# Attention and a gated feed-forward on one core: w_in without its scaling copy, the first job's probabilities kept in float32, four blocks of x turned by TensorE, and a new order

## The chip, the core and the metric

The kernel runs on one core of a Trainium2 chip. A core has five engines that run side by side: TensorE (PE in the profile, with its weight loads as PEld), VectorE (DVE), ScalarE (ACT), GpSimd (POOL) and SyncE (SP), which here issues nearly all the transfers. The metric is device time in microseconds (us), lower is better.

## What is computed

The reference takes q, k and v of four batches, eight heads, 1152 rows and 64 columns, and two matrices of a feed-forward network.

```python
q_pool = q.reshape(B, H, S // 2, 2, D).mean(axis=3)
scores = (1 / sqrt(D)) * q_pool @ k.T            # 576 x 1152 a head
attn = softmax(scores)
x = concat_heads(attn @ v)                       # 2304 x 512
h = x @ w_in                                     # 512 -> 2048
out = (h * sigmoid(h)) @ w_out                   # 2048 -> 512
```

Inputs and output are float32. Most products are made in float16, with each operand split into a high part and a rest ("hi" and "lo"), so that three float16 products stand for one of nearly float32 precision.

## The kernel before

**Jobs.** Attention goes by pairs of heads (16 pairs, four a batch). A job is one pair and one chunk of 128 pooled query rows: its two sides are the two heads. A batch has four whole chunks for each pair, and a job of the 64 rows left over for every two pairs: 72 jobs, numbered from 0 here. For each side, TensorE makes the scores into a PSUM tile S (L723), VectorE takes the row maximum (L784, tile nm), and ScalarE the exponential with the row's sum (L800, tile p32, "p" in the profile). There is one S buffer for each side, so that a job's scores can only begin when the exponentials of the job before are done. The first four pairs, which are those of jobs 0 to 17, have their scores made in float32.

**Turning p.** The product with v needs p turned. As a rule p is split into hi (a cast on ACT at L408 or on DVE at L412) and lo (a subtraction at L432 on POOL or DVE), tile phl, and the two halves go through DMA transposes that SP issues (L827), into pt. For side 1 of jobs 0 to 3 TensorE turns p itself: nine float32 transposes into PSUM tiles pp (L841), from which ACT copies hi (L687) and DVE subtracts lo (L432, pt<-pp). Either way 27 float16 products per side follow (L935, tile po). `whole`, which turns a side and keeps it in float32, is in the kernel before but not used.

**Weights.** w_in and w_out come in 32 pieces of 128x512 (16 each), as 64-bit words; ACT and DVE rebuild the float32 value in place (tiles wide and raw): the low word (L613 on ACT or L619 on DVE), a scaled copy into a PSUM tile mm (L606), and the joining of the two on DVE (L634). For w_in a scaling copy in place follows (the `more` step), and for both the hi part (a cast to the weight tile w, by ACT, DVE or POOL) and the lo part (a subtraction at L432 on POOL or DVE).

**Blocks.** When the jobs of a chunk are done, its 128 rows of x are a block. For the first two blocks TensorE turns x (L1064, tile px), and ACT or DVE takes hi (L690 for DVE) and DVE lo (L1085) from PSUM. For the others x is split into xs (ACT or DVE, then POOL or DVE) and turned by a DMA transpose (L1044). A block has 192 products with w_in (L1130), the gate on ACT and DVE (tiles t and g), and 48 with w_out (L1225). 18 blocks in all.

**What sets the order.** All steps are entered in a plan (`Plan.add`) with a cost, a priority, and the tiles that they hold; `Plan.order` then lists them once, at build time, as if each engine took the ready step of least priority number, with a rule for which engine takes a step that several may do. The list is the program: on the chip every engine works through its own instructions in that order, and so does the SP queue. The priorities and the rules' weights are the tables PRI, PRE, W, EV and the constants above them. Steps that use the SBUF ports that DVE and POOL share are entered with port=True.

## Time and profile before

| what | value |
|---|---|
| median of 3 runs | 714.14 us (712.02 to 714.36) |
| the profiled execution | 714.45 us, its span 712.5 us |
| TensorE busy | 653.3 us, 92% of the span |
| ScalarE, VectorE, GpSimd busy | 480.4, 471.9 and 463.9 us, 66 to 67% |
| mean granted clock of TensorE | 0.976 |

The span runs from the first instruction to the last; the execution's own time is 1.95 us longer. All terms below are worked out against the profiled execution, which is 0.31 us above the median. A share of busy time over the whole span mixes stretches that have different limits, so the profile has to be read in stretches: the first 130 us, where TensorE is often idle, and the rest, where it hardly is.

### The profile page before, as it was taken

How to read it: one execution, taken by the hardware profiler on the slowest of the kernel's cores; microseconds unless marked ns; L12 is line 12 of the kernel's file. 1: busy time of each engine (PE TensorE's matmuls, PEld its weight loads, DVE VectorE, ACT ScalarE, POOL GpSimd, SP SyncE). 2: the span in 40 equal slices, each digit the busy share in tenths (PEclk: the TensorE clock that was granted, in tenths of full speed). 3: DMA queues.
4: the chain of work that ended last, by engine and by line, in shares of the span. 5: the costliest groups of instructions: out<-in, count | busy, mean ns of one | idle time of the engine just before them, and what ended most of it. 6: DMA issues, size and time to landing. Idle time of an engine off the chain costs nothing. (4 is left out here: it accounts for less than half of the span.)

```text
span 712.5 us, 23295 instructions
## 1 busy us (share of the span) xinstructions
PE 653.3 (92%) x10052; PEld 470.7 (66%) x10052; DVE 471.9 (66%) x839; ACT 480.4 (67%) x707; POOL 463.9 (65%) x260
## 2 busy tenths in 40 slices
PE   4656877999899999999899999998999999999997
PEld 2333655676767686767486868585868686858767
DVE  5878885689678575776678756586777565754111
ACT  4978977997577665777655766695777675865221
POOL 1657985897437776778635867887579776666111
PEclk8788999999999999999999999999999999999999
DMA  8999899999999999999999999999999999999000
GB/s 347 358 283 246 159 205 225 238 195 212 200 303 177 163 182 168 161 247 194 207 255 172 180 181 166 167 252 176 280 218 172 184 173 157 159 175 158 24 16 16
DMA packets 362886, 138.10 MB, mean 194 GB/s; under 512 B 350112, under 2 KB 350368, under 8 KB 362784
## 3 DMA queue, kind: packets, MB, share of 16 engines
q1 hardware_dynamic: 362624, 136.49, 99.6%
q8 instruction: 78, 1.28, 0.7%
q14 instruction: 24, 0.20, 0.1%
q10 hardware_dynamic: 160, 0.13, 0.1%
HBM read 45.09 MB, written 4.72 MB: 70 GB/s over the span
## 5 line engine op out<-in xcount | busy, mean ns | idle before, releaser
L432 POOL TENSOR_TENSOR phl<-p,phl 128x1152 f16<-128x1152 f32 x119 | 291.6, 2457 | 100.6 <-DVE phl L412 58.6
L800 ACT ACTIVATE p<-S,nm 128x1152 f32<-128x1152 f32 x144 | 174.8, 1215 | 99.1 <-DVE nm L791 46.5
L784 DVE TENSOR_REDUCE nm<-S 128x1 f32<-128x1152 f32 x144 | 194.5, 1351 | 53.2 <-PE S L723 52.9
L1130 PE MATMUL mm<-xt,w 128*128 128x128 f16 x3456 | 203.6, 220 | 4.8 <-DVE raw L634 2.1
L1130 PEld LDWEIGHTS <-w 128*128 128x128 f16 x3456 | 195.5, 98 | 11.1 <-DMA xt<-xs 2.5
L1225 PE MATMUL mm<-w,g 128*128 128x512 f16 x816 | 186.5, 380 | 2.1 <-DVE nm L791 1.9
L432 POOL TENSOR_TENSOR g<-t,g 128x512 f16<-128x512 f32 x72 | 98.4, 1368 | 80.4 <-ACT g L408 79.6
L723 PE MATMUL S<-K,Q 64*128 64x512 f16 (+7 forms) x1320 | 138.2, 373 | 13.4 <-ACT p L800 6.7
L935 PE MATMUL po<-V,pt 128*128 128x64 f16 (+1 forms) x4320 | 130.8, 195 | 20.0 <-DMA pt<-phl 9.8
L935 PEld LDWEIGHTS <-pt 128*128 128x128 f16 (+1 forms) x4320 | 122.3, 102 | 32.4 <-issue 12.7
L1225 PEld LDWEIGHTS <-g 128*128 128x128 f16 x816 | 75.9, 98 | 85.7 <-issue 2.5
L408 ACT ACTIVATE phl<-p 128x1152 f16<-128x1152 f32 x99 | 114.4, 1160 | 8.2 <-DMA pt<-phl 5.8
L1151 DVE SCALAR_TENSOR_TENSOR t<-t,mm 128x512 f32<-128x512 f32 x72 | 49.3, 684 | 59.8 <-ACT t L1144 57.6
L723 PEld LDWEIGHTS <-Q 64*128 64x128 f16 (+1 forms) x1080 | 42.2, 97 | 51.3 <-issue 11.1
L1144 ACT ACTIVATE t<-mm 128x512 f32<-128x512 f32 x72 | 42.5, 591 | 23.0 <-PE mm L1130 22.7
L408 ACT ACTIVATE g<-t 128x512 f16<-128x512 f32 x72 | 45.1, 627 | 18.0 <-DVE t L1151 17.9
L761 DVE TENSOR_SCALAR r<-sum 128x1 f32<-128x1 f32 (+1 forms) x152 | 17.1, 147 | 50.5 <-ACT p L800 50.1
L723 PEld LDWEIGHTS S<-K,Q 64*128 64x128 f32 (+1 forms) x240 | 23.2, 211 | 39.4 <-issue 24.2
L412 DVE CAST phl<-p 128x1152 f16<-128x1152 f32 x41 | 33.7, 822 | 9.9 <-DMA pt<-phl 7.1
L432 POOL TENSOR_TENSOR xs<-x,xs 128x512 f16<-128x512 f32 (+1 forms) x16 | 19.8, 1238 | 24.3 <-ACT xs L408 24.1
L432 DVE TENSOR_TENSOR phl<-p,phl 128x1152 f16<-128x1152 f32 x21 | 32.1, 1533 | 4.4 <-ACT phl L408 4.2
L535 DVE SCALAR_TENSOR_TENSOR V<-ld,V 128x1152 f16<-128x1152 f32 x16 | 27.6, 1729 | 6.6 <-ACT V L408 6.6
(59 smaller groups left out, 390.7 us busy)
## 6 DMA issues: line engine op xcount, KB each, us to landing
ld<-q SPq DMA_DIRECT2D x16, 576.0 KB, 5.7
ld<-v SPq DMA_DIRECT2D x16, 576.0 KB, 6.1
ld<-k SPq DMA_DIRECT2D x12, 576.0 KB, 6.4
pt<-phl SPq DMA_TRANSPOSE x280, 4.3
wide<-w_in SPq DMA_DIRECT2D x8, 512.0 KB, 8.8
wide<-w_out SPq DMA_DIRECT2D x8, 512.0 KB, 7.9
raw<-w_in SPq DMA_DIRECT2D x8, 512.0 KB, 4.9
raw<-w_out SPq DMA_DIRECT2D x8, 512.0 KB, 5.4
```

The source lines that it names most:

```text
L408: nc.scalar.activation(out=out(), in_=src(), func=AF.Copy, scale=scale or 1.0)
L412: nc.vector.tensor_copy(out=out(), in_=src())
L432: return lambda: getattr(engine, op)(out=out(), in0=a(), in1=b())
L535: lambda: nc.vector.scalar_tensor_tensor(out=values(1), in0=v3(), scalar=V_SCALE, in1=values(0)[:, :, :D], op0=ALU.mult, op1=ALU.subtract,),
L723: nc.tensor.matmul(o[to, c], lhsT=a[rows, s], rhs=x[rows, c], start=n == 0, stop=n == len(terms) - 1,)
L784: lambda: nc.vector.tensor_reduce(out=nm(), in_=ps()[:, :S], op=ALU.max, axis=AX.X),
L800: lambda: nc.scalar.activation(out=p32(), in_=ps()[:, :S], func=AF.Exp, scale=0.0625, bias=nm(), **({} if SUM_BY_PE else dict(accum_out=sm ...
L935: nc.tensor.matmul(o[to, keep : keep + n], lhsT=pt[:, hl * NK + c, cols], rhs=vv[:, at : at + n], start=c == 0 and hl + vl == 0, stop=c == ...
L1130: nc.tensor.matmul(o, lhsT=w[:, f // 2 % 4, wl, cols], rhs=moving(xl, kk), start=kk == 0 and wl + xl == 0, stop=kk == 3 and wl == 1,)
L1144: lambda: nc.scalar.activation(out=t(), in_=h(), func=AF.Tanh, scale=1.0 / G_SCALE),
L1151: lambda: nc.vector.scalar_tensor_tensor(out=t(), in0=t(), scalar=1.0, in1=h(), op0=ALU.add, op1=ALU.mult,),
L1225: nc.tensor.matmul(o(), lhsT=g[ff // 4]()[:, gl, ff % 4], rhs=w[:, u % 4, wl, e * DM : e * DM + DM], start=ff == ffs[0] and gl + wl == 0, ...
```

## The change

Three edits go with a new set of the planner's tables, and thus with another order of everything.

1. `MORE = False`: the scaling copy of the 16 w_in pieces is left out. The cast to hi takes the scale along, and lo, which was a subtraction on POOL or DVE, is now scalar times value minus hi, one instruction on DVE alone (`LO_BY`).
2. `SIDES32 = 2`: both sides of job 0 go through `whole`. TensorE turns p in float32, ACT or DVE copies it once, and nine float32 products with v as it was loaded take the place of the 27 float16 ones. Side 0 had gone by hi, lo and two DMA transposes; side 1 by nine transposes, hi and lo.
3. `X_BY_PE = 4`: blocks 2 and 3 of x are turned by TensorE, too.

The planner has a new constant `LATE`, which lets it count on the result of a DMA transpose later, and new costs for a few steps. `T_IN_PSUM` is set so that the step at L606 stays as it was.

```diff
-WAIT = 0.189
-AHEAD, SWITCH, STEAL = 1.286, 21.317, 1.144
+WAIT = 0.183
+LATE = 0.781
+AHEAD, SWITCH, STEAL = 3.441, 215.979, 1.229
...
-MORE = True
+LO_BY = ("dve",)
+MORE = False
...
-X_BY_PE = 2
-SIDES32 = 0
+X_BY_PE = 4
+SIDES32 = 2
+T_IN_PSUM = True
...
-            at = max(at, b.end + (0.0 if same else LATENCY[b.engine]))
+            at = max(at, b.end + (0.0 if same else LATENCY[b.engine]) + (LATE if b.moves == "turn" else 0.0))
...
             if more != 1.0:
-                add(
-                    "dve", slow,
-                    lambda: nc.vector.scalar_tensor_tensor(
+                def lo_on(engine):
+                    return lambda: engine.scalar_tensor_tensor(
                         out=w()[:, u % 4, 1, c], in0=value(), scalar=more, in1=hi(),
                         op0=ALU.mult, op1=ALU.subtract,
-                    ),
+                    )
+
+                either(
+                    [x for x in (("dve", slow, lo_on(nc.vector)), ("pool", pool_cost(512), lo_on(nc.gpsimd))) if x[0] in LO_BY],
                     pr + W["lo"], [("raw", *tok), ("whi", *tok)], [("wlo", *tok)], [raw, w],
                 )
...
                 if by_32(j, i):
                     add(
-                        "pe", 9 * 4 * pe_cost(64) + 0.1,
+                        "pe", 2.02,
```

Three places of the new order matter below. In the names, the numbers tell buffers apart.

On the SP queue, after the loads of the first three pairs; before:

```order
L595 DMA wide_129<-w_in 128x1024 x2
L595 DMA wide_129<-w_out 128x1024
L827 DMA_TRANSPOSE pt_175<-phl_161 128x9x128 x2
L474 DMA ld_201<-q 128x1152
L474 DMA K_204<-k 128x1152
L474 DMA ld_215<-v 128x1152
L595 DMA wide_129<-w_out 128x1024
```

and after, at the same place:

```order
L599 DMA wide_129<-w_in 128x1024 x2
L599 DMA wide_129<-w_out 128x1024 x2
L477 DMA ld_175<-q 128x1152
L477 DMA K_181<-k 128x1152
L477 DMA ld_191<-v 128x1152
L599 DMA raw_208<-w_in 128x1024
```

The two transposes of job 0's side 0 are gone, and the loads of the fourth pair (q, k, v) follow the weights directly.

On TensorE, from the last transpose of job 0's side 1 (p_21) on; before, with the scores of job 2 in S_52 and S_53:

```order
L841 MATMUL pp_189<-one_84,p_21_134 128x128
L841 MATMUL pp_220<-one_84,p_43_212 128x128 x4
L841 MATMUL pp_230<-one_84,p_43_212 128x128 x4
L723 MATMUL S_52_242<-K_101,Q_137 128x512
L723 MATMUL S_53_243<-K_101,Q_137 128x512
```

and after, with the scores of job 2 in S_56 and S_57:

```order
L884 MATMUL pp_189<-one_84,p_21_134 128x128
L884 MATMUL pp_195<-one_84,p_25_146 128x128 x4
L884 MATMUL pp_203<-one_84,p_25_146 128x128 x4
L884 MATMUL pp_216<-one_84,p_25_146 128x128
L930 MATMUL po_224<-ld_91,pt_210 128x64 x9
L930 MATMUL po_224<-ld_91,pt_155 128x64 x9
L730 MATMUL S_56_264<-K_101,Q_137 128x512
```

The nine transposes of side 0 (p_25) and the 18 float32 products of job 0 now stand ahead of job 2's scores; the transposes of job 1's side 1 (p_43 before) have moved behind them.

On VectorE, from the reciprocal of job 0's sums to the row maxima of job 1; before:

```order
L773 RECIPROCAL r_157<-r_157 128x2
L412 CAST phl_161<-p_25_146 128x1152
L432 TENSOR_TENSOR pt_155<-pp_141,pt_155 128x512
L432 TENSOR_TENSOR pt_155<-pp_150,pt_155 128x512
L634 SCALAR_TENSOR_TENSOR wide_107<-mm_180,wide_107 128x512
L535 SCALAR_TENSOR_TENSOR V_163<-ld_105,V_163 128x1152
L634 SCALAR_TENSOR_TENSOR wide_107<-mm_184,wide_107 128x512
L432 TENSOR_TENSOR pt_155<-pp_189,pt_155 128x128
L784 TENSOR_REDUCE nm_198<-S_32_166 128x1
```

and after:

```order
L780 RECIPROCAL r_157<-r_157 128x2
L538 SCALAR_TENSOR_TENSOR V_161<-ld_105,V_161 128x1152
L639 SCALAR_TENSOR_TENSOR wide_107<-mm_177,wide_107 128x512
L639 SCALAR_TENSOR_TENSOR wide_107<-mm_183,wide_107 128x512
L791 TENSOR_REDUCE nm_193<-S_31_164 128x1
L798 TENSOR_SCALAR nm_193<-nm_193 128x1
L791 TENSOR_REDUCE nm_214<-S_30_163 128x1
L798 TENSOR_SCALAR nm_214<-nm_214 128x1
L661 SCALAR_TENSOR_TENSOR w_0_36_185<-wide_107,w_0_36_185 128x512 x2
```

Job 0's cast and its three lo subtractions are gone, and the new lo instructions of w_in (L661) have come in behind the row maxima of job 1.

## Rows read from the trace of the kernel before

**Rows 1.** The page: busy time of TensorE, and its busy tenths in 40 slices.

```profile
PE 653.3 (92%) x10052; PEld 470.7 (66%) x10052; DVE 471.9 (66%) x839; ACT 480.4 (67%) x707; POOL 463.9 (65%) x260
...
PE   4656877999899999999899999998999999999997
```

**Rows 2.** Busy time by stretch: us, the engines, then clock, DMA share, GB/s.

```profile
10.00:60.00 50.00, 29.11 (x264) 18.73 (x260) 42.59 (x79) 42.00 (x70) 27.64 (x19) 0.80 1.07 333
60.00:100.00 40.00, 30.89 (x446) 21.67 (x444) 33.72 (x60) 36.29 (x57) 36.10 (x22) 0.91 0.95 181
100.00:130.00 30.00, 23.33 (x348) 17.29 (x347) 19.35 (x37) 22.17 (x35) 21.13 (x13) 0.94 1.13 222
130.00:200.00 70.00, 66.71 (x1036) 46.84 (x1033) 52.29 (x89) 53.19 (x81) 50.07 (x30) 0.98 1.15 216
200.00:650.00 450.00, 440.65 (x7180) 318.30 (x7179) 313.20 (x562) 309.32 (x440) 312.47 (x160) 1.00 1.09 194
```

**Rows 3.** What TensorE waited for in the first 150 us: us, times, longest.

```profile
PE pp L841 <- ACT p L800: 12.6, 4, 4.5
```

**Rows 4.** Groups of instructions, first 150 us: count, busy us, mean ns, idle before.

```profile
L432 POOL TENSOR_TENSOR phl<-p,phl 128x1152 f16<-128x1152 f32 x23 | 56.3, 2456 | 24.7 <-DVE phl L412 14.9 <-ACT phl L408 9.7
...
L408 ACT ACTIVATE phl<-p 128x1152 f16<-128x1152 f32 x16 | 18.4, 1158 | 1.3 <-DMA pt<-phl 1.2
...
L432 POOL TENSOR_TENSOR w<-wide,w 128x512 f16<-128x512 f32 x14 | 16.3, 1177 | 4.8 <-ACT w L408 4.7
...
L606 ACT ACTIVATE mm<-wide 128x512 f32<-128x512 f32 x16 | 9.8, 631 | 0.0
...
L412 DVE CAST phl<-p 128x1152 f16<-128x1152 f32 x9 | 7.5, 837 | 3.9 <-DMA pt<-phl 3.9
...
L408 ACT ACTIVATE wide<-wide 128x512 f32<-128x512 f32 x7 | 4.7, 677 | 1.2 <-DVE wide L634 1.2
...
L417 POOL TENSOR_SCALAR wide<-wide 128x512 f32<-128x512 f32 x1 | 0.6, 641 | 0.1
```

**Rows 5.** DVE instructions by line: count, min/median/max ns (three answers).

```profile
L535 DVE SCALAR_TENSOR_TENSOR V<-ld,V x4: 1348/1377/2308, 8.8 to 35.8; 128x1152 f16<-128x1152 f32 x4
...
L432 DVE TENSOR_TENSOR Q<-ld x2: 750/754/757, 4.8 to 10.1; 128x576 f32<-128x576 f32 x2
L432 DVE TENSOR_TENSOR w<-wide,w x2: 1544/1614/1683, 81.9 to 84.5; 128x512 f16<-128x512 f32 x2
L432 DVE TENSOR_TENSOR w<-raw,w x1: 686/686/686, 91.5 to 91.5; 128x512 f16<-128x512 f32 x1
L432 DVE TENSOR_TENSOR phl<-p,phl x1: 1352/1352/1352, 124.2 to 124.2; 128x1152 f16<-128x1152 f32 x1
...
L619 DVE TENSOR_SCALAR raw<-raw x2: 428/1510/2592, 38.8 to 39.2; 128x512 uint32<-128x512 uint32 x2
```

**Rows 6.** TensorE in order of time: start, us, what [idle before].

```profile
25.33 1.97 PE L841 MATMUL pp<-one,p 128*128 128x128 f32 x8 [4.54 <-ACT p L800]
27.23 3.98 PE L723 MATMUL S<-K,Q 64*128 64x512 f32 x12
...
98.73 0.60 PE L1064 MATMUL px<-one,x 128*128 128x128 f32 x4
...
115.82 2.84 PE L1130 MATMUL mm<-xt,w 128*128 128x128 f16 x48 [0.42 <-DVE x L1007]
...
130.38 2.75 PE L1225 MATMUL mm<-w,g 128*128 128x512 f16 x12 [0.28 <-DVE t L1151]
133.06 2.21 PE L723 MATMUL S<-K,Q 64*128 64x512 f32 x12
```

**Rows 7.** TensorE's weight loads for the float32 transposes, first 60 us, ns.

```profile
L841 PEld LDWEIGHTS pp<-one,p x36: 139/225/231, 14.3 to 52.8; 128*128 128x128 f32 x36
```

**Rows 8.** The SP queue in order of time.

```profile
16.97 8.61 SPq L827 DMA_TRANSPOSE pt<-phl  x2
```

**Rows 9.** ACT's wait on a weight load, 10 to 100 us.

```profile
ACT wide L613 <- DMA wide<-w_in: 1.4, 1, 1.4
```

More of the change, by code (lines that the diff above doesn't have):

```diff
@@ L150, in add @@
         tiles = [x for t in tiles for x in (t, t.share) if x is not None]
-        op = Op(options, priority, tiles, port, moves, matmuls, mode, spare)
+        op = Op(options, round(priority, 4), tiles, port, moves, matmuls, mode, spare)
         before = []
@@ L581, in halves, with carried @@
                 return bits().bitcast(F16).rearrange("p (a b) -> p a b", b=4)[:, :, j]
-            def tu():
-                return t().bitcast(U32)
             def value():
                 return words(1)
+            def carried():
+                return t() if T_IN_PSUM else words(1)
             def hi():
@@ L625, in weights @@
                 "act": ("act", act_cost(512) + 0.02, low_act),
[L626 removed]
+                "dve": ("dve", dve_cost(512, True) + 0.08, low_on(nc.vector)),
             }
@@ L629, in weights @@
                 [ways[x] for x in LOW_BY],
-                pr + W["low"], writes=[("low", *tok)], reads=[("raw", *tok)], tiles=[raw],
+                pr + W["low"], writes=[("low", *tok)], reads=[("raw", *tok) if T_IN_PSUM else ("came", *tok)], tiles=[raw],
             )
@@ L634, in weights @@
                 lambda: nc.vector.scalar_tensor_tensor(
-                    out=words(1).bitcast(U32), in0=tu(), scalar=3, in1=words(0).bitcast(U32),
+                    out=words(1).bitcast(U32), in0=carried().bitcast(U32), scalar=3, in1=words(0).bitcast(U32),
                     op0=ALU.logical_shift_left, op1=ALU.bitwise_or,
                 ),
-                pr + W["put"], [("low", *tok), ("t", *tok)], [("raw", *tok)], [t, raw], port=False,
+                pr + W["put"], [("low", *tok), ("t", *tok)], [("raw", *tok)], [*scratch, raw], port=not T_IN_PSUM,
             )
```

33 lines of the change are left out of this document (17 added, 16 removed).

## The prediction

> **What bounds the kernel now.** I read the page's busy row and its slices first, then the busy time by stretch, then TensorE's waits, and last the groups of instructions. The busy row alone would say that TensorE sets the time at 92%, but the slices show where the missing 8% lie: they are low up to about the seventh and near nine tenths from there to the end [rows 1]. By stretch, TensorE is idle for 20.9 of the 50 us from 10 to 60, for 9.1 of the 40 up to 100, for 6.7 of the 30 up to 130, then for 3.3 of 70 and 9.4 of 450 [rows 2]. From 130 us on it is thus the bound, and whatever it has not done by then is added at the end. Ahead of that it waits, most of all for the exponentials that its float32 transposes need, 12.6 us in four waits [rows 3]. No single engine holds it there: from 10 to 60 VectorE and ScalarE are busy for 85 and 84% and GpSimd for 55%; from 60 to 100 they are at 84, 91 and 90% [rows 2]. The start-up is work of three engines that pass pieces to each other, and GpSimd becomes a bound in its second part.
>
> The mark that I use is the start of job 13's scores, at 133.06 us [rows 6]: ahead of it TensorE is idle often, behind it hardly. The end moves by two things: by how much earlier this mark is reached, and by how much more of TensorE's own work is done when it is.
>
> **What the new order has done by the mark.** Counted in the two orders, TensorE has 48 more products with w_in (288 for 240) and 12 more with w_out (48 for 36) ahead of job 13's scores, and as many jobs' products with v. 48 of the first took 2.84 us and 12 of the second 2.75 [rows 6], together 5.6 us that no longer have to be done behind the mark.
>
> The other engines' work up to the row maximum, the exponential and the split of job 13, as counts by durations:
>
> ScalarE: 9 copies in place fewer, at 0.68 us, -6.1 [rows 4] (all 13 scaling copies that it had go, but more of the low words now stand ahead of the mark); 5 casts to hi fewer, at the same 0.68, -3.4; 4 scaled copies into PSUM more, at 0.63, +2.5; 3 casts of p more, at 1.16, +3.5 [rows 4]; three copies of turned p, x and pieces of the gate more, seven in all at about 0.6 each (the 0.63 of its PSUM copies is the nearest row), +4.0. Sum +0.5.
>
> VectorE: the 16 new lo instructions. Its free subtraction of this size took 0.69 [rows 5], so +11.0; 4 joinings and gates more of that size, +2.8; 4 casts of p fewer, at 0.84, -3.4 [rows 4]; job 0's three lo subtractions, one of w and one copy of x fewer, some 3.1. Sum +7.3.
>
> GpSimd: 12 subtractions of w fewer, at 1.18, -14.1; 3 scaling copies fewer and 9 casts to hi more, at 0.64, +3.8; one subtraction of p fewer, at 2.46, -2.5 [rows 4]; one of the gate more and one of x fewer, 0. Sum -12.8.
>
> Together -5.0 us of work. From 10 to 130 us the three engines did 95.7, 100.5 and 84.9 us of it, 281 in 120 [rows 2], or 2.34 us for each us of time. If they go on at that rate the mark comes 2.1 us earlier. The bounds: if VectorE alone set the pace (it was busy for 80% of the 120 us), its 7.3 us cost 9.2; if GpSimd alone did (71%), its 12.8 give back 18. I take the mean rate, since no engine was the bound throughout.
>
> **What else is added.** The new lo instructions read two operands from SBUF, as the lo step of v does, and that one took 2.31 us for 1.35 where GpSimd was at work beside it [rows 5]. Of the ten two-operand SBUF instructions that VectorE ran in the first 150 us (four on v, three on w, two on q, one on p), three were so held up, v once by 0.96 and w twice, to 1.54 and 1.68 for 0.69 [rows 5]; that is 2.8 us over ten, 0.28 each. For sixteen this is 4.5 us of VectorE, and at 2.34 a us of time 1.9. The longest hold that the trace shows is 2.16 (2.59 for 0.43, a low word) [rows 5], so the range for all sixteen runs from nothing to 34.6 us of VectorE.
>
> The Trainium skill, SBUF — State Buffer, Who interferes with whom, says that a VectorE instruction with two SBUF inputs and a GpSimd one that reads SBUF exclude each other for the whole of the one that came first. The trace agrees, by the 2.31 us above. Taken as chance meetings with a GpSimd that is busy 71% of the time from 10 to 100 us and in the middle of a 2.46 us subtraction, the rule would give an estimate of 0.87 us a hold and a time of 712.2 instead of the forecast below; I hold to the measured 0.28, because it is of this kind of order.
>
> Job 0. Side 0 loses its cast, its subtraction and two DMA transposes. SP stood at those from 16.97 to 25.58, and the fourth pair's loads only went out behind them [rows 8]; now they follow the weights. What this gives back is bounded by nothing below (no engine is shown to wait for the q or k of that pair) and by the waits on loads: ScalarE's 1.4 us for a piece of w_in [rows 9]. I take the 1.4, since a queue without the two transposes lets those pieces go out earlier, too. TensorE gets nine transposes (eight took 1.97 at the low clock [rows 6]) and 18 float32 products for 54 float16 ones. The trace has no such product; its float32 weight loads took 139 to 231 ns, median 225 [rows 7], so by those 18 cost 2.5 to 4.2 us, and twice as much, 8.4, if the load is not what counts and the clock is low (scores took 3.98 at 27 us and 2.21 at 133 [rows 6]). They stand ahead of job 2's scores, which wait behind them, and so do the row maxima of job 2. I cost them at nothing: TensorE sat idle for 4.54 us just there, from 20.8 to 25.3, until job 1's exponentials [rows 6], and had no other work. If that cover is gone or the clock is low, they delay the start-up by up to 4 us. Below nothing they can't go: what they spare the other engines is counted above.
>
> Blocks 2 and 3 of x: eight transposes, which come behind the mark, where TensorE is the bound. Four took 0.60 in the midst of other work [rows 6]: +1.2. The split and the two DMA transposes that go lie beside TensorE's work, where the other engines are busy for 70 to 75% [rows 2], and count for nothing.
>
> Behind 200 us the counts of each engine barely change, TensorE was idle for 9.4 of 450 us [rows 2], and the new order may make that a few us more or less: 0, with 3 either way.
>
> **The sum.** -5.6 (work done earlier) -2.1 (three engines) +1.9 (holds) -1.4 (transfers) +1.2 (x) = -6.0. From 714.45 that is 708.45; the median of the runs stood 0.31 lower, so 708.1.
>
> **Rivals.**
>
> VectorE becomes the bound (slower). It is the one engine that gets work, 7.3 us and the holds, up to the mark. Against it: it was idle for a fifth of the time there, and the row maxima depend on TensorE and ScalarE. For it: 84 to 85% up to 100 us [rows 2]. Then 7.3 and 4.5 us come at 80% busy: 14.8 us later, less 5.6 and 1.4 and with 1.2: 723.1. In holds alone: each us of mean hold costs 16 / 2.34 = 6.8 us, the sum without holds is 706.5 for the profiled execution, and so this alone makes it slower by over 0.3% (716.6) from 1.5 us a hold on.
>
> The start-up is set by transfers and by the one score buffer (no change). Each job's scores wait for exponentials, and the DMA queues' share is 0.95 to 1.13 in all of these stretches [rows 2]; only two of the many transposes go. Then neither the relief nor the earlier weights show, and what is left is 1.2 less 1.4: 713.9.
>
> The float32 products stand in the way: at the low clock, 4 us behind the exponentials of job 1, so 712.1.
>
> **How the numbers follow.** A measurement of this kernel can tell about 0.3%, 2.1 us. The forecast's case has a chance of 0.60, and its own range is 701 to 712. VectorE as the bound has 0.14, no change 0.14, the products in the way 0.12, half of it faster and half within 0.3%. So faster is 0.66, same 0.20, slower 0.14. The range leaves out most of VectorE's case and the best tenth of a relief that GpSimd's bound makes larger: 700 to 715.5.
>
> **What would show it.** In the profile after, job 13's scores should begin at about 131 us, with the idle time of TensorE from 10 us to there down from 37 to some 29 us; GpSimd's share from 60 to 100 should fall from 90% to below 80. The new lo instructions should take 0.7 us in the main, and 1.5 or more in a quarter of cases. Job 2's scores should begin at 27 to 28 us; 31 would say that the float32 products are in the way. Work behind 200 us should have 6 to 12 us of idle TensorE time. The prediction is wrong if the row maxima come later from VectorE's own queue, or if idle time behind 200 us grows by more than the start-up gains.

## The result, and the profile after

The changed kernel is slower. Its median is 720.59 us (718.66 to 721.74, four runs) against 713.71 us for the kernel before beside it; the ratio is 1.0097, with an interval of 1.0068 to 1.0127. The forecast was 708.1, and its range, 700 to 715.5, doesn't hold the result.

| | before | after |
|---|---|---|
| median | 713.71 us | 720.59 us |
| profiled execution, its span | 714.45, 712.5 us | 718.66, 716.8 us |
| TensorE busy | 653.3 us | 657.4 us |
| start of job 13's scores | 133.06 us | 141.98 us |

The page of the changed kernel, which answers to [rows 1], shows nearly the same picture: 92% busy, low ahead of the eighth slice, nine tenths behind it.

```profile
span 716.8 us, 23264 instructions
...
PE 657.4 (92%) x10051; PEld 475.5 (66%) x10051; DVE 464.7 (65%) x833; ACT 479.5 (67%) x697; POOL 461.8 (64%) x258
...
PE   4665887999899999999899999999899999999997
```

The busy time by stretch, with the columns of [rows 2]: the time, then PE, PEld, DVE, ACT and POOL, the clock, the DMA share, GB/s.

```profile
10.00:60.00 50.00, 30.64 (x241) 20.52 (x238) 40.42 (x75) 42.55 (x72) 20.14 (x17) 0.85 1.06 340
60.00:100.00 40.00, 30.90 (x384) 20.91 (x385) 32.39 (x61) 30.67 (x46) 29.60 (x20) 0.84 0.86 166
100.00:130.00 30.00, 23.13 (x306) 17.53 (x304) 21.11 (x39) 22.57 (x36) 18.37 (x10) 0.95 1.06 196
130.00:200.00 70.00, 65.31 (x1029) 46.83 (x1029) 52.26 (x93) 52.39 (x76) 52.67 (x28) 1.00 1.08 202
200.00:650.00 450.00, 440.57 (x7220) 317.69 (x7215) 303.10 (x545) 310.00 (x439) 321.12 (x165) 1.00 1.09 193
```

GpSimd's share from 60 to 100 us fell from 90 to 74% and ScalarE's from 91 to 77%, as was meant, and TensorE was idle there for 9.1 us, as before [rows 2]. The relief is real, and nothing came of it.

Cut at the start of job 13's scores, the mark of the prediction, the kernel before gives these two rows (same columns):

```profile
0.00:133.06 133.06, 89.83 (x1070) 60.60 (x1071) 98.96 (x181) 105.97 (x169) 87.26 (x61) 0.88 1.03 258
133.06:712.50 579.44, 563.52 (x8983) 410.07 (x8982) 372.98 (x658) 374.42 (x540) 376.59 (x200) 1.00 1.00 179
```

and the changed one these:

```profile
0.00:141.98 141.98, 100.13 (x1121) 69.60 (x1121) 104.27 (x189) 108.38 (x169) 75.79 (x55) 0.89 0.99 246
141.98:716.80 574.82, 557.27 (x8930) 405.86 (x8930) 360.45 (x645) 371.12 (x528) 386.00 (x203) 1.00 0.99 178
```

Behind the mark the changed kernel needs 574.82 us for 579.44, 4.6 less. Ahead of it TensorE does 10.3 us more work, and is idle for 41.9 us, where it was idle for 43.2. So the idle time of the start-up, in which the additional products were to be hidden, has hardly shrunk: the mark came 8.9 us later, and 8.9 less 4.6 is the 4.3 us by which the span grew. (The medians lie 6.9 us apart; the profiled execution of the changed kernel is the fastest of its four.)

TensorE in order of time, which answers to [rows 6]:

```profile
23.44 4.23 PE L930 MATMUL po<-ld,pt 128*128 128x64 f32 x36 [0.16 <-ACT pt L694]
27.60 2.21 PE L730 MATMUL S<-K,Q 64*128 64x512 f32 x12
...
108.39 0.61 PE L1071 MATMUL px<-one,x 128*128 128x128 f32 x4
113.85 2.85 PE L1137 MATMUL mm<-xt,w 128*128 128x128 f16 x48
...
139.19 2.75 PE L1232 MATMUL mm<-w,g 128*128 128x512 f16 x12
141.98 2.21 PE L730 MATMUL S<-K,Q 64*128 64x512 f32 x12
```

TensorE's waits in the first 150 us, which answer to [rows 3] (wait, us, times, longest): the transposes wait less for the exponentials, 4.2 us for 12.6, and the scores wait 8.0 for 5.7 before.

```profile
PE S L730 <- ACT p L807: 8.0, 4, 2.7
...
PE pp L884 <- ACT p L807: 4.2, 1, 4.2
```

Job 2's scores still begin on time (27.60 for 27.23). The time is lost later: from job 4's scores to job 8's it took 34.4 us before (49.97 to 84.41) and 45.9 after (48.20 to 94.08). The timeline of the changed kernel at job 5 shows one such place. A row is start, duration, engine, line, instruction, and in brackets the idle time before it with its releaser.

```profile
60.02 3.86 DVE L661 SCALAR_TENSOR_TENSOR w<-wide,w 128x512 f16<-128x512 f32 x2
...
60.77 2.57 POOL L435 TENSOR_TENSOR phl<-p,phl 128x1152 f16<-128x1152 f32 x1 [0.20 <-ACT phl L411]
...
61.94 4.11 PE L730 MATMUL S<-K,Q 64*128 64x512 f32 x12 [2.62 <-ACT p L807]
...
67.79 1.35 DVE L791 TENSOR_REDUCE nm<-S 128x1 f32<-128x1152 f32 x1
...
69.06 0.68 DVE L639 SCALAR_TENSOR_TENSOR raw<-mm,raw 128x512 uint32<-128x512 uint32 x1
69.65 0.14 DVE L798 TENSOR_SCALAR nm<-nm 128x1 f32<-128x1 f32 x1
...
69.91 1.22 ACT L807 ACTIVATE p<-S,nm 128x1152 f32<-128x1152 f32 x1 [0.68 <-DVE nm L798]
...
71.25 1.16 ACT L411 ACTIVATE phl<-p 128x1152 f16<-128x1152 f32 x1
...
72.33 1.20 ACT L807 ACTIVATE p<-S,nm 128x1152 f32<-128x1152 f32 x1
```

The scores end at 66.05, but VectorE takes the row maximum only at 67.79: two of the new lo instructions (L661) took 3.86 us, one of them held while GpSimd's subtraction (L435) ran, and what had queued behind them ran first. Between the maximum and its scale stands a joining of w (L639), and between the two exponentials a cast of p (L411). Job 6's scores could begin at 73.67.

### The profile page after: what moved, and what is told of

Same layout as the page of the kernel before. It is cut to its first block, busy times and chain, and to the rows that moved or that the text cites. A ratio compares the mean times of both kernels' runs of the same rounds, so it can differ in the third digit from the quotient of the medians.

```text
span 716.8 us, 23264 instructions
## 1 busy us (share of the span) xinstructions
PE 657.4 (92%) x10051; PEld 475.5 (66%) x10051; DVE 464.7 (65%) x833; ACT 479.5 (67%) x697; POOL 461.8 (64%) x258
## 4 chain that ended last, share of the span: by engine, by line
PE 42%; POOL 4%; DMA 4%; issue 3%; DVE 2%; SPq 2%; ACT 1%; POOLq 0%; ACTq 0%; DVEq 0%
PE mm L1137 14%; PE mm L1232 13%; PE po L942 7%; PE S L730 7%; DMA pt<-phl 3%; POOL phl L435 2%; PE mm L1185 1%; POOL g L435 1%; DMA ld<-k 1%; SPq L834 1%; DVE nm L791 1%; DVE K L435 1%; ACT p L807 1%; POOL Q L435 0%; SPq L477 0%
## 5 line engine op out<-in xcount | busy, mean ns | idle before, releaser
L435 POOL TENSOR_TENSOR phl<-p,phl 128x1152 f16<-128x1152 f32 x124 | 305.1, 2468 | 119.7 <-ACT phl L411 74.4
L435 POOL TENSOR_TENSOR g<-t,g 128x512 f16<-128x512 f32 x72 | 96.4, 1340 | 64.5 <-ACT g L411 63.9
L942 PE MATMUL po<-V,pt 128*128 128x64 f16 (+1 forms) x4266 | 128.2, 194 | 10.6 <-DMA pt<-phl 4.0
L411 ACT ACTIVATE phl<-p 128x1152 f16<-128x1152 f32 x107 | 123.8, 1162 | 10.4 <-DMA pt<-phl 5.3
L411 ACT ACTIVATE g<-t 128x512 f16<-128x512 f32 x72 | 45.2, 628 | 18.4 <-DVE t L1158 18.3
L1014 DVE TENSOR_TENSOR x<-po,r 128x128 f32<-128x128 f32 x72 | 20.6, 287 | 28.2 <-PE po L942 26.1
L538 DVE SCALAR_TENSOR_TENSOR V<-ld,V 128x1152 f16<-128x1152 f32 x16 | 32.6, 2036 | 7.2 <-ACT V L411 7.2
L807 ACT ACTIVATION_READ_ACCUMULATOR p<-S,nm 128x1 f32 x144 | 28.2, 196 | 0.0
L415 DVE CAST phl<-p 128x1152 f16<-128x1152 f32 x32 | 25.6, 800 | 2.3 <-ACT p L807 1.1
```

Of the source, the lines that this page charges most:

```text
L411: nc.scalar.activation(out=out(), in_=src(), func=AF.Copy, scale=scale or 1.0)
L415: nc.vector.tensor_copy(out=out(), in_=src())
L435: return lambda: getattr(engine, op)(out=out(), in0=a(), in1=b())
L538: lambda: nc.vector.scalar_tensor_tensor(out=values(1), in0=v3(), scalar=V_SCALE, in1=values(0)[:, :, :D], op0=ALU.mult, op1=ALU.subtract,),
L807: lambda: nc.scalar.activation(out=p32(), in_=ps()[:, :S], func=AF.Exp, scale=0.0625, bias=nm(), **({} if SUM_BY_PE else dict(accum_out=sm ...
L942: nc.tensor.matmul(o[to, keep : keep + n], lhsT=pt[:, hl * NK + c, cols], rhs=vv[:, at : at + n], start=c == 0 and hl + vl == 0, stop=c == ...
```

## The experiments

"Fixed order" means that a kernel's planned list is kept and only the named steps are moved, with `behind(x, y)`: x, and the steps between that need it, come behind y. The table has the start of some jobs' scores in each run's profile, and the medians with their ratio to the kernel before.

| run | job 2 | 4 | 5 | 8 | 13 | median, ratio (interval) |
|---|---|---|---|---|---|---|
| before | 27.2 | 50.0 | 58.0 | 84.4 | 133.1 | 713.7 |
| after | 27.6 | 48.2 | 61.9 | 94.1 | 142.0 | 720.6, 1.0097 (1.0068 to 1.0127) |
| as_changed_again | 27.2 | 48.6 | 62.2 | 94.2 | 141.3 | 720.9, 1.0110 (1.0050 to 1.0169) |
| edits_old_tables | 32.4 | 55.3 | 72.7 | 103.1 | 144.8 | 731.7, 1.0261 (1.0225 to 1.0296) |
| new_tables_no_edits | 27.9 | 49.4 | 63.1 | 99.2 | 140.1 | 731.7, 1.0257 (1.0230 to 1.0284) |
| loads_behind_transposes | 28.0 | 55.9 | 67.6 | 97.9 | 144.8 | 724.8, 1.0160 (1.0107 to 1.0212) |
| raws_behind_transposes | 30.2 | 51.7 | 64.0 | 96.0 | 144.0 | 719.1, 1.0073 (1.0044 to 1.0102) |
| products_behind_scores | 25.8 | 51.8 | 62.7 | 95.0 | 141.3 | 722.3, 1.0114 (1.0068 to 1.0160) |
| filler_for_the_clock | 28.0 | 52.9 | 62.9 | 95.0 | 140.7 | 719.6, 1.0082 (1.0051 to 1.0112) |
| casts_behind_exponentials | 32.0 | 53.6 | 63.5 | 94.5 | 140.4 | 718.5, 1.0047 (1.0017 to 1.0078) |
| chain_cleared | 30.5 | 53.6 | 62.3 | 97.7 | 145.2 | 721.1, 1.0109 (1.0057 to 1.0160) |
| lo_as_zeros | 27.3 | 48.0 | 61.7 | 92.3 | 138.5 | 717.5, 1.0036 (1.0011 to 1.0061) |
| copy_put_back | 29.1 | 52.3 | 63.9 | 95.8 | 144.6 | 721.1, 1.0104 (1.0068 to 1.0140) |
| new_lo_on_gpsimd | 27.4 | 48.1 | 62.1 | 92.0 | 139.3 | 718.3, 1.0038 (1.0008 to 1.0069) |
| low_words_on_scalar_new | 27.4 | 49.6 | 62.4 | 93.5 | 138.8 | 717.0, 1.0033 (1.0005 to 1.0062) |
| lo_on_gpsimd_and_casts | 27.3 | 48.1 | 61.1 | 95.4 | 138.9 | 716.2, 1.0012 (0.9991 to 1.0032) |
| first_edit_alone | 28.8 | 51.6 | 58.9 | 89.0 | 134.7 | 721.1, 1.0107 (1.0056 to 1.0158) |
| first_edit_lo_off_the_chain | 27.0 | 51.4 | 58.9 | 87.0 | 137.2 | 723.5, 1.0110 (1.0089 to 1.0131) |
| copies_left_out_only | 27.6 | 50.2 | 59.2 | 85.1 | 133.7 | 715.5, 1.0010 (0.9992 to 1.0028) |
| low_words_on_scalar_old | 28.2 | 50.5 | 59.9 | 86.4 | 134.9 | 717.2, 1.0041 (1.0015 to 1.0066) |

The last four keep the old order, as edits_old_tables keeps the old tables. The medians were taken on several chips, on which the kernel before had 713.1 to 715.5, so the ratio is what to compare. A profile is one execution: from job 13's scores to the end the five profiles of the old order took 579.4 to 585.2 us and the thirteen of the changed order 572.1 to 581.1, so a few us between two profiles there show nothing by themselves.

**Edits and tables apart.** First the obvious split: the three edits with the old tables, and the new tables without the edits, each planned anew. The edit of the second:

```diff
-MORE = False
+MORE = True
...
-X_BY_PE = 4
-SIDES32 = 2
+X_BY_PE = 2
+SIDES32 = 0
```

> The three edits under the planner's tables of before (the new constant for transposes set to 0), so another order than that of either kernel. Theory P (the order that the new tables make puts waits into the chain of scores, row maximum and exponential; the edits themselves are good for the 5 to 6 us of w_in, p and x work that they spare): 705 to 712 us, job 13's scores at 130 to 134 us. Rival E (the edits cost, by the lo instructions that VectorE now has alone): 717 us or more, job 13's scores at 138 us or later.

> The new tables with all three edits undone: scaling copy of w_in back, job 0 by float16, two blocks of x turned by TensorE. Theory P: as slow as after or slower, 718 to 726 us, since the tables make the order. Rival E: 710 to 715 us, since the costly edits are gone.

Both took 731.7, 18 us more than before, and so neither theory holds in both. The row of the long stretch shows about half of it: TensorE, which was idle there for 9.4 us before and after, is idle for 19.1 in the first and 18.4 in the second. The mark, at 144.8 and 140.1 us for 133.1, adds 11.8 and 7.0.

```profile
200.00:650.00 450.00, 430.94 (x7051) 310.78 (x7049) 314.43 (x554) 294.88 (x422) 298.45 (x155) 1.00 1.10 191
```

```profile
200.00:650.00 450.00, 431.62 (x7032) 311.33 (x7030) 316.81 (x553) 299.08 (x426) 305.08 (x155) 1.00 1.07 192
```

It seems that a set of tables fits the steps that it was made for; in any case these two runs measure a new order each, and not the edits. All further runs keep an order and change single steps in it.

**Transfers.** Job 2's second pair of transposes is issued at 40.93 behind six weight loads, and ScalarE then waits 3.5 us for the buffer that it frees. Four of the loads, and then only the two that are used last, were put behind those transposes.

```diff
+for n in (10, 11, 20, 21):
+    behind(named["load", n], named["turn", 2, 0, 1])
```

> After, its planned order kept, but four of the six weight loads (2 MB) that stand on the SP queue ahead of the two transposes of job 2's side 0 are moved behind them, with the steps that need them. In the trace of after the second transpose lands at 51.84 us, ScalarE's copy of job 3's turned p waits until 51.97 for the buffer it frees, and VectorE, GpSimd and TensorE stand behind for 2.6 to 4.5 us. Theory Q (that wait is worth its 3.5 us in the score chain): 715 to 718 us, the copy at 49 us or earlier, job 5's scores at about 58.5 in place of 61.9. Rival (the weights come later instead and give it back): 719 to 722 us.

> The changed kernel in its fixed order, and only two of the six weight loads that stood ahead of job 2's second half of transposes (the two of 0.5 MB each that are first used some 20 steps later) issued behind them. Theory W (the wait for those transposes, 3.5 us of ScalarE at 48.5 to 52.0, lengthens the chain scores, row maximum, exponential, next scores): the second half lands about 2 us earlier, the stretch from job 4's to job 8's scores falls from 45.9 to 43 to 44.5, and the time from 720.6 to 718.5 to 720. Rival D (the transposes are late by their own speed, whatever stands ahead of them): the landing stays at 50 to 52 us, and the time within 1 us of 720.6.

The first was no faster (724.8; its interval overlaps that of the changed kernel): ScalarE now waited for a moved load, with job 3's exponential behind it.

```profile
52.47 0.67 ACT L619 ACTIVATE wide<-wide 128x512 int32<-128x512 uint16 x1 [7.94 <-DMA wide<-w_out]
53.02 1.21 ACT L808 ACTIVATE p<-S,nm 128x1152 f32<-128x1152 f32 x1
```

In the second the transposes left SP's queue at 47.6 instead of 49.9, but job 8's scores began at 96.0, no earlier than before the edit, and the ratio, 1.0073, can't be told from 1.0097. Theory W's own figures came in: 2.3 us earlier, 44.3 us from job 4's to job 8's scores, and 719.1. So this wait may be worth one or two of the 6.9 us, which these runs can't tell from nothing; it is not the bulk of them.

**The float32 products.** They were put behind job 2's scores.

```diff
+for i in (1, 0):
+    behind(named["sums", 0, i], named["score", 2])
```

> The changed kernel in its fixed order, with the 18 float32 products of job 0 (4.23 us at the high clock, 7.7 at the low one) behind job 2's scores instead of ahead of them. Theory F (they hold the chain up at the very start, and by more in executions in which the clock is low there, which is also why the changed kernel's times scatter): job 2's scores start at 25.5 to 27 in every execution instead of 27.6 or 32.0, the spread falls, and the time is 716 to 719. Rival G (the chain is given time back at jobs 3 to 8 whatever job 2 does, since transposes and weights set their pace, and job 1's transposes, now behind the products, come later by 2.6 to 6 us): within 1 us of 720.6, or up to 723.

Job 2's scores came at 25.79, 1.8 us earlier, job 3's at 42.41 for 38.70: job 1's transposes now stand behind the products. The median went up, if anything. G holds.

```profile
25.79 3.87 PE L731 MATMUL S<-K,Q 64*128 64x512 f32 x12 [2.77 <-ACT p L808]
29.58 4.23 PE L931 MATMUL po<-ld,pt 128*128 128x64 f32 x36
34.20 1.25 PE L849 MATMUL pp<-one,p 128*128 128x128 f32 x8 [0.39 <-DVE x L1015]
```

**The clock.** Float16 products whose result is overwritten were to fill TensorE's wait ahead of the transposes of jobs 2 to 5.

```diff
+if j in (2, 3, 4, 5) and i == 1 and c == 0:
+    x = one().bitcast(F16)
+    for _ in range(16):
+        nc.tensor.matmul(ps()[:, :256], lhsT=x[:, :P], rhs=x, start=True, stop=True)
```

> The changed kernel in its fixed order, with 16 more f16 products of 256 columns, whose result is overwritten, ahead of the first transpose of side 1 in each of the jobs 2, 3, 4 and 5, where TensorE otherwise waits for the exponential (1.7 us of work at the high clock, 3.4 at the low one). Theory K (the low granted clock lengthens the scores of jobs 3 to 6, 3.8, 3.7, 4.1 and 4.2 us for 2.1 at the high clock, and these stand in the chain): two or three of these four scores fall to 2.1 to 3, the stretch from job 3 to job 7 shortens by 3 to 5 us, and the time is 716 to 719. Rival H (the clock follows the chain's waits and is no cause, or the filler holds the transposes up by what it gives to the scores): within 1.5 us of 720.6, or up to 724.

Jobs 3 and 4 had their scores at the high clock (2.21 us for 3.78 and 3.73). But at job 2 the filler did not fill the wait: it began when the wait of 4.02 us was over, and held job 2's transposes up by its own 3.6 us. Job 8's scores came at 95.0. H holds: 1.0082 is within the uncertainty of 1.0097. What a higher clock would give without that hold-up was not tried: the granted clock from 60 to 100 us is 0.84 in the profile of the changed kernel, for 0.91 before.

```profile
36.89 3.60 PE L850 MATMUL pp<-one 128*128 128x256 f16 x16 [4.02 <-DVE wide L639]
40.28 1.85 PE L852 MATMUL pp<-one,p 128*128 128x128 f32 x8
42.06 2.21 PE L730 MATMUL S<-K,Q 64*128 64x512 f32 x12
```

**The casts between the exponentials.**

```diff
+for j in range(4, 8):
+    behind(named["cast", j, 1], named["exp", j, 0])
```

> After, its planned order kept, but in jobs 4 to 7 ScalarE's cast of side 1's p goes behind the exponential of side 0 instead of between the two. Theory C (the cast holds the exponential that the next job's scores wait for, by 1.0 to 2.0 us in each of three to four jobs): 715 to 717.5 us, job 8's scores at about 91 in place of 94.1. Rival (the cast only fills time in which the second row maximum isn't ready, and side 1's transposes come later by as much): 719 to 722 us.

Measured: 718.5, ratio 1.0047. In its profile the exponentials stand together (before the edit 1.16 us of cast stood between them):

```profile
70.35 1.22 ACT L808 ACTIVATE p<-S,nm 128x1152 f32<-128x1152 f32 x1 [0.69 <-DVE nm L799]
...
71.72 1.22 ACT L808 ACTIVATE p<-S,nm 128x1152 f32<-128x1152 f32 x1
...
72.94 1.15 ACT L412 ACTIVATE phl<-p 128x1152 f16<-128x1152 f32 x1
```

From job 4's to job 8's scores it took 40.9 us for 45.9. In that one execution the start was late (float32 products at the low clock, 7.7 us), so that job 8's start, 94.5, shows no gain. The median lies between the two forecasts, half a per cent below the changed kernel's, with intervals that overlap (1.0017 to 1.0078 and 1.0068 to 1.0127).

**The chain, all of it.** If the chain scores, maximum, exponential, next scores set the start-up by itself, whatever stands in it should count.

```diff
+for j in range(3, 13):
+    for x, y in (
+        (("top", j, 1), ("scale", j, 1)), (("top", j, 0), ("scale", j, 0)), (("exp", j, 1), ("exp", j, 0))
+    ):
+        x, y = named[x], named[y]
+        for o in order[order.index(x) + 1 : order.index(y)][::-1]:
+            if o.engine == x.engine and order.index(o) < order.index(y):
+                behind(o, y)
```

> The changed kernel in its fixed order, but for the jobs 3 to 12 whatever stands on VectorE between a side's row maximum and its scale (mostly one put of 0.6 to 0.7 us), and on ScalarE between a job's two exponentials (a cast of 1.1 to 1.2 us, at job 7 also a copy and an activation of 0.6 each, later ones like it), is moved behind the second of the two; nothing is left out. Theory C (the serial chain scores, row maximum, exponential, next scores sets the start-up, so what stands in it counts in full): jobs 4 to 8 lose 4 casts of 1.1 and some 3 or 4 puts of 0.6, some 6 us, and the later jobs some 3 more; job 13's scores come at 132 to 137 instead of 142, and the time is 712 to 716. Rival A (something outside the chain, the transfers until 60 us and the words of the weights that all three engines must still make before the products, sets the moment at which job 8 and job 13 can come; work taken out of the chain comes back as waits): job 8's scores stay at 93 to 96 as in all the runs so far, job 13's at 139 or later, and the time at 718 or more.

> The changed kernel itself, nothing edited, for a second profile and more times beside the other experiments. Both theories: 720.6, within 719 to 722; start of job 2's scores either near 27.6 (float32 products at the high clock, 4.2 us) or near 32 (at the low one, 7.7 us); job 8's scores at 93 to 96 in either case if rival A holds, 4 us later in the second if theory C alone holds.

It doesn't: 721.1, and job 13's scores at 145.2, though the same casts at jobs 4 to 7 were among what was moved. The steps taken out of the chain came back as waits at other places; ScalarE, for one, now waits for a load of w_out that had not held it up at that place:

```profile
90.57 0.68 ACT L619 ACTIVATE raw<-raw 128x512 int32<-128x512 uint16 x1 [3.49 <-DMA raw<-w_out]
91.15 0.58 ACT L1152 ACTIVATE t<-mm 128x512 f32<-128x512 f32 x1
```

The table says the same: in the changed order job 5's scores begin at 61 to 64 us in every run but that with four loads moved, whether job 4's began at 48 or at 53.6, while the four runs in the old order have them at 59 to 60. So the theory of the chain alone falls. The changed kernel itself, run again, gave 720.9.

**VectorE's new work.** First the low half of w_in as zeros by VectorE's memset.

```diff
-return lambda: engine.scalar_tensor_tensor(
-    out=w()[:, u % 4, 1, c], in0=value(), scalar=more, in1=hi(), op0=ALU.mult, op1=ALU.subtract)
+return lambda: engine.memset(w()[:, u % 4, 1, c], 0.0)
```

> The changed kernel with the low half of w_in written as zeros by VectorE's memset instead of computed (this leaves the low half of w_in out of the result; the instructions stay in number and place, each some 0.2 to 0.3 us instead of 0.69, and read neither the raw words nor the high half). Theory W (the chain sets the start-up, VectorE has slack; of the new work only the holds stand in the chain): the one hold of 2.2 us ahead of job 5's row maximum goes, and some of the 16 x 0.4 us: 717 to 719.5. Rival V (VectorE became the bound through the 16 new instructions): all 16 x 0.45 = 7 us come off the start-up: 713 to 715.

717.5, ratio 1.0036: some 4 to 5 us come back for 10.6 us of VectorE (16 instructions took 15.0 us, and 4.4 as memsets). The median is in theory W's range and not in V's: not all of this work was in the way. In the profile VectorE is then busy for 96.9 us ahead of the mark, less than the 99.0 before the change, and the mark still comes at 138.5:

```profile
0.00:138.52 138.52, 99.37 (x1122) 67.59 (x1122) 96.88 (x191) 107.85 (x170) 75.44 (x55) 0.89 1.00 251
```

Then the first edit by itself, in the old order, and taken back by itself, in the new one.

```diff
+def lo_now():
+    nc.vector.scalar_tensor_tensor(
+        out=w()[:, u % 4, 1, c], in0=value(), scalar=more, in1=hi(),
+        op0=ALU.mult, op1=ALU.subtract,
+    )
...
-order = plan.order()
+order = [op for op in plan.order() if op not in left_out]
```

```diff
+nc.scalar.activation(out=value(), in_=value(), func=AF.Copy, scale=more)
...
+return lambda: nc.gpsimd.tensor_sub(out=w()[:, u % 4, 1, c], in0=value(), in1=hi())
```

> The kernel before, its planned order kept as it is, with the first of the three edits alone: w_in's scaling copies are not issued (their places on the three engines stay empty), the high half is cast with the scale, and the low half is computed from the two by VectorE at the place where GpSimd's or VectorE's subtraction stood. P in float32 and the two further blocks of x are as before. Theory O (the edits are right, and the new order, not the new work, loses the time): the engines have 16 x 0.7 us less of copies and GpSimd 16 x 1.2 us less, VectorE more; no wait is new, so the time is 709 to 713.5, below the kernel before. Rival E (the 16 new VectorE instructions are what costs, in whatever order): 716 to 721.

> The changed kernel, its planned order kept as it is, with the first edit alone taken back: a scaling copy of w_in on ScalarE ahead of each high half (16 x 0.65 us), and the low half by GpSimd's subtraction (16 x 1.15 us) at the place of VectorE's (16 x 0.69 us, one of them held to 2.9). Theory O (the order loses the time): no better than the changed kernel, 720 to 725, since ScalarE has 10 us more to do in the same order. Rival E (the new VectorE instructions cost it): 714 to 718.

The first edit alone costs 7.6 us (1.0107), as much as the whole change. ScalarE's exponentials now wait for VectorE's scale of the maximum, 11.2 us in the stretch from 10 to 140 us (wait, us, times, longest), where the kernel before has 0.2 us of it:

```profile
ACT p L803 <- DVE nm L794: 11.2, 9, 3.4
```

Cut at job 13's scores, this profile is longer on both sides: by 1.65 us ahead, and by 5.75 behind, where TensorE is idle for 21.1 us instead of 15.9.

```profile
0.00:134.71 134.71, 92.34 (x1070) 62.22 (x1070) 108.00 (x193) 99.71 (x157) 69.15 (x44) 0.85 1.03 253
134.71:719.90 585.19, 564.07 (x8982) 410.32 (x8982) 378.55 (x663) 373.88 (x538) 373.31 (x197) 1.00 0.99 178
```

How much of the loss lies on either side is not shown by that: copies_left_out_only, below, whose median is that of the kernel before, took 583.8 us behind the mark in its profile, an execution 4 us above its median. The last of the new lo instructions ran at 157 us, behind the mark.

Putting the copy back gave nothing (1.0104): over the span VectorE was busy for 11.7 us less, ScalarE for 8.7 and GpSimd for 16.6 more. That result fits theory O, the first run rival E; to part the three engines, w_in was scaled by 2^8 (v and x by 2^2 for 2^6 in exchange), so that lo is a plain subtraction without any copy, and the place of VectorE's instructions was tried, too.

```diff
-V_SCALE = 2.0**6
-X_SCALE = 2.0**6
-W_IN_SCALE = 2.0**4
+V_SCALE = 2.0**2
+X_SCALE = 2.0**2
+W_IN_SCALE = 2.0**8
```

> The kernel before, its planned order kept, with w_in scaled by 2^8 as w_out is, and v and with it x by 2^2 for 2^6, so that no scaling copy is needed and the low half stays a plain subtraction where it was: the 16 copies (13 on ScalarE, 3 on GpSimd, 10.9 us) are not issued, nothing is added or moved, and nothing is left out of the result. Theory V (VectorE's work between the scores and the exponentials sets the start-up; relief of ScalarE and GpSimd is worth little): 711.5 to 714. Mean-rate rule of the prediction (each us of any of the three engines is worth 1 / 2.34): 10.9 / 2.34 = 4.7 less, 708 to 710.5. Rival P (any departure from what an order was planned for costs): 716 or more.

> The changed kernel, its planned order kept, with the same scales (w_in by 2^8, v and x by 2^2), so that the low half of w_in is a plain subtraction, and this on GpSimd (16 x 1.15 us) at the place of VectorE's instruction (16 x 0.69 and its holds, 14.4 us in all); no copy, nothing left out of the result. Theory V: VectorE is relieved of what lay in the chain, GpSimd has room (74% busy from 60 to 100 us): 716 to 719, as with the low half left out (717.5). Mean-rate rule: 4 us of work more, 722. Rival P: 720 to 722, no change, as in the run with the copy put back, where ScalarE had 10.6 us more.

> The kernel before in its planned order with the first edit alone, as the run of that name (721.1), but the 8 of its 16 new VectorE instructions that stand between a side's row maximum and its scale come behind the scale; nothing else. Theory V with the place deciding: 8 x 0.69 us and the holds among them come off the way to the exponentials, 715 to 718. Rival T (VectorE's total decides, wherever the instructions stand, since the next row maximum waits for them instead): 720 to 722.

These three say where the cost lies. The 16 copies taken off ScalarE and GpSimd, with nothing added, are worth nothing: 1.0010, where the mean-rate rule asked for 0.993, and job 13's scores at 133.7. This run and the first edit alone keep the same order and both do without the copies; they differ in how lo is made, and with VectorE's instructions it takes 1% more. The same lo work on GpSimd instead of VectorE, in the changed order, gives 0.6% back (1.0038) though GpSimd is then busy for 97% from 60 to 100 us. And moving 8 of the 16 instructions behind the scale, in the old order, gives nothing (1.0110), though ScalarE's wait for the scale falls from 11.2 to 6.1 us: neither that place nor that wait sets the time, and theory V's part on the place falls. That VectorE's total counts wherever it stands (rival T) fits, but isn't shown apart: four of the eight then stand between the two sides' row maxima (at 34.83, 81.73, 91.30 and 109.64 us), still ahead of the second exponential. The two rows of the run on GpSimd:

```profile
0.00:139.31 139.31, 99.08 (x1121) 68.81 (x1121) 94.84 (x174) 108.26 (x169) 94.34 (x71) 0.90 0.99 252
139.31:711.40 572.09, 557.24 (x8930) 405.76 (x8930) 359.38 (x644) 371.00 (x528) 386.94 (x204) 1.00 1.00 178
```

Next to the changed kernel, VectorE has 9.4 us less ahead of the mark and GpSimd 18.6 more; TensorE's idle time falls by 1.6 us ahead of the mark and by 2.7 behind it (in an execution 5 us below the median of its run).

**The other direction.** If VectorE's work sets the pace, taking more of it away should help. The 13 low-word steps that it did went to ScalarE, at the same place.

```diff
-"dve": ("dve", dve_cost(512, True), low_on(nc.vector)),
+"dve": ("dve", dve_cost(512, True), low_act),
```

> The run with the copies left out only (715.5, the old order), and the 13 low-word steps that VectorE did (12 of them in the first 140 us, 7.9 us there, four of them held up) are done by ScalarE at the same place, 0.68 us each; nothing is left out of the result. Theory V (VectorE's total work sets the start-up, at about half a us of time for each us): 3 to 5 us less than 715.5, 710 to 713, below the kernel before. Rival S (the exponentials' engine is as much in the chain as VectorE; what is moved from the one to the other gives nothing): 714 to 717.

> The run with the new low halves on GpSimd (718.3, the changed order), and VectorE's low-word steps done by ScalarE at the same place. Theory V: 3 to 5 us less, 713 to 715.5. Rival S: 717 to 720.

It does not, in the old order (1.0041 after 1.0010) nor clearly in the new (1.0033 after 1.0038). Rival S holds: ScalarE is as near to being the bound as VectorE is. Two runs in the changed order give it a number: copy_put_back and new_lo_on_gpsimd both have lo on GpSimd, and the first has 16 copies on ScalarE that the second has not (117.0 us of ScalarE ahead of the mark for 108.3). 1.0104 for 1.0038: 8.7 us put on ScalarE cost about what 10.6 us taken off VectorE gave back.

**Both repairs.**

> The changed kernel in its order with both: the new low halves by GpSimd (as the run new_lo_on_gpsimd, 718.3) and the casts of side 1 behind side 0's exponential at jobs 4 to 7 (as the run casts_behind_exponentials, 718.5); nothing left out. If they are two causes that add: 715.5 to 717. If they are one, or the time taken out of the chain comes back as other waits: 717.5 to 720. The kernel before stands at 714.

716.2, ratio 1.0012 (0.9991 to 1.0032): together they come to 0.9% of the 1.0% that the change had cost, as if the two added, and the kernel is where it was before, not below it. The step from 1.0038 to 1.0012 by itself isn't clear of noise, so the casts' part is likely and not shown.

## Why the prediction was wrong

**Where TensorE is the bound, the terms came out.** The forecast for the part behind the mark was -5.6 (products done ahead) +1.2 (eight transposes of x), -4.4; it measured -4.6 in the first profile and -3.8 in the second (575.68 us). That it came so close is in part luck, since single executions differ by more. TensorE's idle time from 200 to 650 us is 9.4 us, as before, in the range named. Of the work up to the mark, GpSimd's -12.8 measured -11.5 and ScalarE's +0.5 is +2.4; VectorE's +7.3, with 4.5 of holds, is only +5.3.

**The step that failed is the mark.** Job 13's scores were to come about 2 us earlier, at 131, by two steps: the work taken off the three engines, at one price for all, and room in TensorE's idle time for all that TensorE got more. They came at 142.0, and neither step held.

**The price of the three engines' work.** The prediction took their sum, -5.0, at the mean rate of 2.34 us for each us, as if a us of GpSimd were worth a us of VectorE, and got -2.1; GpSimd's -12.8 stood in it as 5.5 us of gain. The runs show other prices. In the changed order, 10.6 us off VectorE gave some 4.8 back (1.0103, the mean of the changed kernel's two ratios, to 1.0036) and 8.7 onto ScalarE cost about as much, near half a us for each us, not far from the mean rate's 0.43. But 18.6 us onto GpSimd with 9.4 off VectorE gave 4.6 back, where the mean rate asks for 3.9 more: VectorE's share at its price is 4.2 of it, and no cost is left for GpSimd, though it was busy for 97% from 60 to 100 us. In the old order, 10.9 us of copies off ScalarE and GpSimd gave nothing, and VectorE's 16 instructions cost 1%. So work off GpSimd was no gain. The reason to take the mean, "no engine was the bound throughout", was the mistake: VectorE and ScalarE were busy for 85 and 84% from 10 to 60 us [rows 2], both in the chain through which each job's scores come, and GpSimd for 55%. But the price is not all: without GpSimd the same rule gives +3.3 in place of -2.1, and the sum is -0.6, no change.

**The rival that came nearest.** VectorE as the bound, at 723.1 with a chance of 14%, is nearest to the measured time, but its mechanism isn't what the runs show: VectorE got 5.3 us ahead of the mark and not 11.8, and with its new work as zeros it does less there than before the change, with the mark at 138.5. That the mark came 8.9 us later, near the 9.2 of the bound "if VectorE alone set the pace", is luck.

**The cover for TensorE's new work.** The 60 products done ahead, 18 float32 products for 54 float16 ones and nine transposes were put into TensorE's idle time at no cost: idle from 10 us to the mark was to fall from 37 us to 29. It fell to 35.7 (by the rows of the mark, less the first 10 us), while TensorE's work ahead of the mark grew by 10.3 us. The edits to single causes leave the mark at 138.5 us or later in the changed order. With both repairs it is at 138.9, 5.8 us later than before; TensorE does 8.9 us more ahead of it, and is idle for 40.2 us for 43.2:

```profile
0.00:138.87 138.87, 98.69 (x1121) 68.37 (x1121) 95.35 (x173) 108.28 (x169) 94.28 (x71) 0.90 1.00 250
```

So most of that work was not hidden, whatever engine made lo. Whether TensorE's products themselves lengthen the start-up or the new order makes other waits wasn't tried apart, and stays open.

**The new order's own part.** The prediction counted what the order moved, not what it put between two steps of one chain. Four casts between exponentials may cost some 0.5%, by the median of their run; that run's interval overlaps the changed kernel's, and the run that moved them together with more showed no gain.

**Holds** were sized right in all, but not in their spread. The 16 instructions, in two groups (line, instruction, count, busy, mean ns):

```profile
L661 DVE SCALAR_TENSOR_TENSOR w<-wide,w 128x512 f16<-128x512 f32 x8 | 7.9, 1006 | 0.6 <-POOL w L420 0.5 <-ACT w L411 0.2
L661 DVE SCALAR_TENSOR_TENSOR w<-raw,w 128x512 f16<-128x512 f32 x8 | 7.1, 900 | 1.0 <-POOL w L420 1.0
```

15.0 us in all, for 16 at 0.69, or 0.25 us of hold each (0.28 forecast). Of the four that were to take 1.5 us or more there was one. It took 2.85 us, while GpSimd's subtraction ran from 60.77 to 63.34. The Trainium skill's rule (SBUF — State Buffer, Who interferes with whom) agrees in kind, by that row; its use as chance meetings, 0.87 each, is over three times too much.

**Transfers** (-1.4). The wait itself went: ScalarE no longer waits for a piece of w_in from 10 to 100 us. But in that stretch it now waits 3.5 us for the buffer that job 2's transposes free, and no run shows a gain: neither order of the loads behind the transposes was faster by more than the noise.

**Job 0** was costed at nothing, with 4 us if the clock is low. In the first profile the products took 4.23 us and job 2's scores came at 27.60; in another execution they took 7.7 and the scores came at 32.0. But neither this nor their place sets the time, as the run with the products moved shows.

**Blocks of x.** One cost was missed: the first product of the last of these blocks waited 2.2 us for VectorE's part of xt at 194 us. It is within the 4.6 us behind the mark.

So the sum was -6.0, and the change +6.9. The new VectorE work and the casts together account for 6.5, the difference between 1.0103 and 1.0012; the forecast had +1.9 for it, the holds, and counted the instructions themselves in its -2.1. The -2.1 and the -1.4 are gains that no run shows. With -4.4 for the part behind the mark that makes +2.1, and the 4.8 us that are left would be the cover's, by the rows above; no run settled that.

## What to carry to other kernels

Where engines pass pieces to each other in a chain, price a us of work by the engine that it is on: take it off one engine alone, in an unchanged order, and measure, before a mean over engines is used as a rate. Here work moved from an engine with room to one that is busy for 85% was a loss even though the sum fell. Idle time in a start-up that waits on such a chain is no sure cover for more work either: here it hardly shrank. And when the order is planned anew with an edit, count what stands between the steps of the chain, since the plan and the edits could not be measured apart here by recombining them.

## What was not expected of the hardware

Eighteen float32 products of 128x128 by 128x64 took 4.23 us at a granted clock of 1.00, 0.235 each and in 36 records, and 7.71 in an execution in which it was 0.54 there; 54 float16 products of the same size took 1.74. The clock of the first 30 us differs between executions: with those products in the changed order's place, job 2's scores began at 27.2 to 32.0 us. And job 2's second pair of transposes left the queue at 49.1 to 50.7 us in the eleven profiles that keep the changed order's loads, wherever between 40.8 and 45.7 it was issued, with the DMA share above 1.0 up to 60 us: a transfer issued earlier behind those loads was not done earlier. With two of the six loads moved behind them they left at 47.6.
